# Rows of attention divided and rounded pair by pair on GpSimd, and five engines in program order

## The chip, the cores and the metric

The kernel runs on one core of one Trainium2 chip. The metric is device microseconds of a whole execution: the median of three runs was 1037.98 us (1031.45 to 1040.16). The core has TensorE (matrix products), VectorE, ScalarE, GpSimd and SyncE, each with an instruction queue of its own; in the profile they are PE, DVE, ACT, POOL and SP, and PEld is TensorE loading weights. SP issues most DMAs, ScalarE's queue issues the loads of Q, K and V, and GpSimd's queue the indirect ones.

## The reference

Attention with a threshold, followed by a mixture of experts in which each token goes to the one expert with the highest logit.

```python
# q, k, v: (8, 8, 576, 64)
scores = scale * (q @ k.T)
thresh = max(scores, axis=-1) - tau
scores = where(scores >= thresh, scores, -1e9)
attn = exp(scores - max(scores)); attn = attn / (sum(attn) + 1e-9)
x = (attn @ v) laid out as (4608, 512)          # 8 heads x 64 per token
logits = x @ w_gate                              # 8 experts
e = argmax(logits); gate = softmax(logits)[e]
out[token] = gate * (relu(x @ w1[e]) @ w2[e])
```

## The kernel before

**Tiling.** The 64 heads are worked on as 32 pairs of heads, four pairs to a batch entry (a batch in what follows, 0 to 7). A pair takes ten steps; step k of the attention loop issues one unit of transposed scores of pair n (`st_unit`: two matmul passes, an exp on ScalarE, a mask on VectorE), one unit of scores of the next pair (`s_unit`, with a row maximum on VectorE) and one piece of attention times V of the pair before (`av_piece`). Numbers are held as a high and a low half in 16 bits, so a split goes with nearly every operand: ScalarE makes the high half, VectorE or GpSimd subtracts it to get the low one. Lines: `lo` of Q and K on GpSimd (L218), the low half of V in `vop` on VectorE (L252), the low half of the exps on GpSimd (L367).

**The row maxima.** When the last score unit of a pair is done, `parts` takes the maximum of its nine columns, transposes them on TensorE (L304), splits them in three and sends them with three DMAs into the operand `CQ` that the next pair's transposed scores need (L318). `stack` copies the split Q and K with eleven or twelve DMAs of SP into the operands (L232 to L247).

**The end of a batch.** When the last of a batch's four pairs has left PSUM, `finish` takes the reciprocals of the sums (L442) and divides and splits the batch in blocks of 128 tokens by 512 columns, four blocks, five in every other batch (the rest of 64 tokens of two batches makes one). For each block `one` multiplies on GpSimd (L456; in the last batch three blocks on VectorE), ScalarE makes the high half (L463), GpSimd the low one (L464), both in the row buffer `R`, and SP transposes the block by DMA (L471). `logits` multiplies the transposed blocks with the gate's weights, `route` finds the expert and the running count (L516 to L527), `ranks` each token's position (L531 to L548), and each block is sent by an indirect DMA of GpSimd to its place in the DRAM buffer `xs` (L556). `R` is one buffer of five blocks, `xT` holds transposed ones.

**The experts.** After batch 5, 6 and 7 `tables0`, `tables1` and `tables2` find which blocks of 128 tokens are whole, and `fetch` brings a block back from `xs` (L756) and transposes it (L759). `gemm1` and `gemm2` (L804, L831) run over 32 blocks and a few late ones. Weights are loaded by SP and split by ScalarE and VectorE (L722, L723).

**Order.** The program plans everything by steps: `after(k, f, where)` puts f into the step k from now, at its front, middle or end; `phase(p, least)` gives the next step that is p modulo ten. PSUM has five score banks, two for attention times V and one (`ps_m`) that L304's transpose, the logits, the ranks and the tables take in turn. Up to step KM = 304, which is 16 before the end of the 320 steps, the queue of TensorE keeps program order; the other engines' queues are put in order by the planner of the language, which runs a timeline of its own. After KM it orders all five.

```python
        with tc.manual_schedule(engines={mybir.EngineType.PE}):
            while k < KM:
                one_step()
```

## Time and profile before

| | |
|---|---|
| median of 3 runs | 1037.98 us (1031.45 to 1040.16) |
| the profiled execution | 1028.81 us, its span 1027.1 us |
| mean granted TensorE clock | 0.978 |
| busy: PE, PEld | 933.3, 662.2 us |
| busy: DVE, ACT, POOL | 685.9, 612.2, 493.9 us |

The rows below are of this one execution. Times in a row are microseconds from the span's start. "PEclk" is the granted clock of TensorE as a share of 2.4 GHz, which is the upper of its two levels; the lower is 1.2. In a timeline the idle time of an engine just before an instruction stands in brackets at the end, with what ended it. A name such as L252 is a line of the kernel.

### The profile page before, as it was taken

To read this page: it belongs to the slowest core of one execution; us is meant where nothing else is said; L and a number is where in the kernel's file an instruction comes from. 1 tells how busy PE (TensorE), PEld (TensorE's weight loads), DVE (VectorE), ACT (ScalarE), POOL (GpSimd) and SP (SyncE) were. 2 spreads that over 40 slices of the span, in tenths; PEclk is the share of its full clock that TensorE was granted. 3 is DMA by queue.
4 is the path that set the end of the run, shared out by engine and by line. 5 is a ranking of instruction groups with operands and counts; after the bars stand their busy time and mean duration, and the time that the engine had idled before them with its cause. 6 is when DMAs were issued, how large, how long until landed. Compare 5 with 4: busy or idle time off the path is not lost.

```text
span 1027.1 us, 25249 instructions
## 1 busy us (share of the span) xinstructions
PE 933.3 (91%) x10027; PEld 662.2 (64%) x10027; DVE 685.9 (67%) x1316; ACT 612.2 (60%) x1002; POOL 493.9 (48%) x411
## 2 busy tenths in 40 slices
...
GB/s 199 141 130 114 105 154 103 148 156 115 157 152 116 141 149 122 181 122 118 121 148 136 86 134 305 285 117 249 235 161 158 234 141 178 160 155 219 218 101 26
DMA packets 181716, 158.97 MB, mean 155 GB/s; under 512 B 137561, under 2 KB 153947, under 8 KB 181596
## 3 DMA queue, kind: packets, MB, share of 16 engines
...
## 4 chain that ended last, share of the span: by engine, by line
PE 48%; DMA 20%; DVE 10%; issue 8%; ACT 7%; POOL 3%; SPq 2%; POOLq 0%; ACTq 0%; DVEq 0%
PE h L804 15%; PE y L831 12%; DMA qkf<-in_qk_dram 5%; DMA CQ<-hi 4%; PE av L405 4%; PE st L330 3%; PE s L281 3%; PE st L331 3%; PE s L283 3%; DMA wf<-in_w_dram 2%; DMA out_dram<-o,gt 2%; DVE nm L293 2%; DVE vop L252 2%; DVE e L361 2%; PE av L399 2%
## 5 line engine op out<-in xcount | busy, mean ns | idle before, releaser
L367 POOL TENSOR_TENSOR pl<-e,ph 128x1024 f16<-128x1024 f32 x95 | 202.7, 2135 | 130.7 <-ACT ph L366 54.3
L293 DVE TENSOR_REDUCE nm<-s 128x1 f32<-128x512 f32 (+1 forms) x320 | 200.3, 633 | 29.9 <-PE s L283 27.9
L804 PEld LDWEIGHTS <-wb 128*128 128x128 f16 x2304 | 191.1, 99 | 31.5 <-issue 10.6
L804 PE MATMUL h<-xTm,wb 128*128 128x256 f16 (+2 forms) x2112 | 197.6, 256 | 12.5 <-DMA xTm<-R 10.1
L831 PE MATMUL y<-wb,hl 128*128 128x512 f16 (+1 forms) x1056 | 203.9, 362 | 0.0
L281 PE MATMUL s<-QK 128*128 128x512 f16 (+3 forms) x640 | 139.5, 295 | 37.2 <-DMA QK<-lo 19.2
L831 PEld LDWEIGHTS <-hl 128*128 128x128 f16 (+1 forms) x1056 | 94.4, 100 | 99.0 <-issue 4.1
L723 DVE SCALAR_TENSOR_TENSOR wb<-wf,wb 128x1024 f16<-128x1024 f32 x96 | 116.5, 1252 | 58.3 <-ACT wb L722 56.8
L358 ACT ACTIVATE e<-st,ntau 128x512 f32<-128x512 f32 x192 | 130.3, 684 | 40.6 <-PE st L331 35.0
L330 PE MATMUL st<-QK 128*128 128x512 f16 (+3 forms) x640 | 138.0, 292 | 11.1 <-DVE e L361 8.2
L283 PE MATMUL s<-ck,CQ 128*128 128x512 f16 (+3 forms) x640 | 143.8, 293 | 1.8 <-DMA QK<-hi 1.8
L361 DVE SCALAR_TENSOR_TENSOR e<-st,e 128x512 f32<-128x512 f32 x192 | 129.8, 678 | 18.3 <-ACT e L358 17.3
L331 PE MATMUL st<-CQ,ck 128*128 128x512 f16 (+3 forms) x640 | 132.9, 289 | 3.4 <-DMA CQ<-ptT 3.4
L792 ACT ACTIVATE hl<-h 128x512 f16<-128x512 f32 (+1 forms) x80 | 45.7, 573 | 120.9 <-PE h L804 120.9
L722 ACT ACTIVATE wb<-wf 128x1024 f16<-128x1024 f32 x96 | 97.7, 1050 | 33.3 <-DMA wf<-in_w_dram 17.7
...
L405 PE MATMUL av<-vf,e 128*128 128x65 f32 (+1 forms) x1024 | 116.3, 251 | 0.0
L343 DVE SCALAR_TENSOR_TENSOR e<-st,e 128x512 f32<-128x512 f32 (+1 forms) x160 | 91.8, 586 | 22.4 <-ACT e L342 21.7
L342 ACT ACTIVATE e<-st,ntau_f 128x512 f32<-128x512 f32 (+1 forms) x160 | 93.6, 605 | 20.5 <-PE st L331 19.2
L366 ACT CAST ph<-e 128x1024 f16<-128x1024 f32 x96 | 99.8, 1039 | 7.8 <-DVE e L361 7.2
L405 PEld LDWEIGHTS av<-vf,e 128*128 128x128 f32 (+1 forms) x1024 | 101.4, 165 | 0.4 <-issue 0.4
L409 PE MATMUL av<-vop,pl 128*128 128x65 f16 x768 | 98.3, 195 | 0.5 <-DVE pl L367 0.3
...
## 6 DMA issues: line engine op xcount, KB each, us to landing
...
```

Of the source, the lines that this page charges most:

```text
L281: nc.tensor.matmul(sc[rows, oc], d["QA"][a][:, cols], d["KB"][a][:, CH[c]], start=True, stop=False)
L283: nc.tensor.matmul(sc[rows, oc], d["CQ"][:, at:at + cols.stop - cols.start], d["CK"][a][:, CH[c]], start=False, stop=True,)
L293: nc.vector.tensor_reduce(o, sc[:, 0:width(t)], axis=AX.X, op=ALU.max, negate=True)
L330: nc.tensor.matmul(sc[rows, oc], d["KB"][a][:, cols], d["QA"][a][:, CH[c]], start=True, stop=False)
L331: nc.tensor.matmul(sc[rows, oc], d["CK"][a][:, cols], d["CQ"][:, q], start=False, stop=True)
L358: nc.scalar.activation(pf, sc, AF.Exp, bias=ntau, scale=0.125 / SS)
L361: nc.vector.scalar_tensor_tensor(pf, sc, 0.0, pf, ALU.is_ge, ALU.mult)
L367: (nc.vector if (n, t) in PLV else nc.gpsimd).tensor_tensor(l, pd, h, ALU.subtract)
L405: nc.tensor.matmul(av[rows, a], d["Pf"][t][:, q], vf[:, tv], start=False, stop=last)
L723: nc.vector.scalar_tensor_tensor(o[:, :, 1], x, SW, o[:, :, 0], ALU.mult, ALU.subtract)
L804: nc.tensor.matmul(o, Wt[:, c, wh, f], x, start=c == 0 and z == 0, stop=c == 3 and z == 2,)
L831: nc.tensor.matmul(o, h[:, hh], Wt[:, f, wh, c], start=f == 0 and z == 0, stop=f == 7 and z == 2)
```

## The change

A pair is divided and rounded as soon as it has left PSUM. `evac` copies attention times V to `y`, `divide` takes the reciprocals of that pair and multiplies on GpSimd (on VectorE for the very last pair), `rounded` has ScalarE write the high half and the same engine the low half straight into the pair's columns of the row buffer. The half block of two batches is done in `lone`. `finish` is left with the transposes (`turn`), one a step, from seven steps after the batch's last pair has left PSUM (two in the last batch), and with the logits. The row buffer is doubled (`Rs`, `Rh`, `xhs`). The low half of V goes from one VectorE instruction to two of GpSimd. In `route` the count `got` moves into PSUM, and nine instructions go three to a step in place of two (`dense`). L304's transpose comes three steps after its maximum instead of two, the logits and ranks sit in the seventh step of a pair instead of the sixth, the exp buffer of tag `pf` has three places instead of four. And the program's order holds for all five queues up to KM.

The diff, without the hunks that only tell `fetch` which row buffer it may use, and that drop a name no longer used:

```diff
--- before.py
+++ after.py
@@ -44,7 +44,7 @@
 CAP = NTOK
 
 TUNE = dict(
-    lead=10, cast=1, sl=8, ll=15, sp0=6, sps=0, lv=-9, sv=-2, av=2, g=3, l=3, d=3, lg=2, g5=3, l5=3, d5=2, g6=1, l6=2, d6=2, g7=1, l7=1, d7=1, off=2, off5=1, off6=11, lg7=13, km=16, rate=15, dh=1, do=3, ws0=6, wsd=3, w1d=5, plv=1, xv=3, so=0, sto=0, ord=0, sc=5, fa=3, fd=4, wa1=-70, wa2=-86, wl1=-28, wl2=-6, avb=2, route=1, ranks=7, pp=8, ew=4, maskat=0, w1a=-40, w1b=3,
+    lead=10, cast=1, sl=8, ll=15, sp0=6, sps=0, lv=-9, sv=-2, av=2, tr=4, d=2, lg=5, d5=2, d6=2, d7=1, lg7=9, km=16, rate=15, dh=1, do=3, ws0=6, wsd=3, w1d=5, plv=1, xv=3, so=0, sto=0, ord=0, sc=5, fa=3, fd=4, wa1=-70, wa2=-86, wl1=-28, wl2=-6, avb=2, route=1, ranks=7, pp=8, ew=4, maskat=0, w1a=-40, w1b=3,
 )
 
 
@@ -191,6 +191,11 @@
             i += slot[0] > FRONT and k == 0
             after(k + i // 2, f, END if i % 2 else MID)
 
+    def dense(k, where, fs):
+
+        for i, f in enumerate(fs, where):
+            after(k + i // 3, f, i % 3)
+
     def due(k, where):
         slot[0] = where
         q = acts.get(k)
@@ -249,9 +254,9 @@
     def split_v(n):
         vop, x = vops[n % NB], vfs[n % NB][:, 0:NV, 0:D]
         nc.scalar.activation(vop[:, :, 0:D], x, AF.Copy, scale=SV)
-        after(1, lambda: nc.vector.scalar_tensor_tensor(
-            vop[:, :, D + 1:2 * D + 1], x, SV, vop[:, :, 0:D], ALU.mult, ALU.subtract
-        ))
+        full = op.tile([P, NV, D], F32, tag="full", name=f"full_{n}", bufs=2)
+        nc.gpsimd.tensor_scalar(full, x, SV, None, ALU.mult)
+        after(1, lambda: nc.gpsimd.tensor_tensor(vop[:, :, D + 1:2 * D + 1], full, vop[:, :, 0:D], ALU.subtract))
 
     def blocks(t):
 
@@ -319,7 +324,7 @@
                     st[n]["CQ"][64 + p:65 + p].rearrange("p (t c) -> p t c", t=9), t[:, p]
                 )
 
-        after(2, turn, FRONT)
+        after(3, turn, FRONT)
 
     def st_unit(n, t):
         d = st[n]
@@ -336,7 +341,7 @@
             elif "pe" in d:
                 pf = d.pop("pe")[:, 1]
             else:
-                d["pe"] = pp.tile([P, 2, 512], F32, tag="pf", name=f"e_{n}_{t}", bufs=4)
+                d["pe"] = pp.tile([P, 2, 512], F32, tag="pf", name=f"e_{n}_{t}", bufs=3)
                 pf = d["pe"][:, 0]
             d["Pf"][t] = pf
             nc.scalar.activation(pf, sc, AF.Exp, bias=ntau_f, scale=0.125 / SS)
@@ -369,15 +374,17 @@
         return mask
 
 
-    xt = {}
     sent = set()
     W = D + 1
-
-    def x_tiles(b):
-        if b not in xt:
-            half = xt[b - 1][1] if b % 2 else xp.tile([P, H, W], F32, tag="xh", name=f"xh_{b}")
-            xt[b] = (xp.tile([P, NT, H, W], F32, tag="x", name=f"x_{b}"), half)
-        return xt[b]
+    Rs = [rpool.tile([P, NT, ROW], I32, name=f"R_{i}") for i in range(2)]
+    Rh = [rpool.tile([P, ROW], I32, name=f"Rh_{i}") for i in range(2)]
+    xhs = [rpool.tile([P, H, W], F32, name=f"xh_{i}") for i in range(2)]
+
+    def row(b, j):
+        return Rs[b % 2][:, j] if j < NT else Rh[b // 2 % 2]
+
+    def halves(x):
+        return x.bitcast(F16).rearrange("p (c h d) -> p c h d", c=4, h=2)
 
     def av_piece(n, a, i):
 
@@ -409,75 +416,96 @@
             nc.tensor.matmul(av[rows, a], l, vop[:, tv, 0:W], start=False, stop=False)
             nc.tensor.matmul(av[rows, a], h, vop[:, tv, 0:W], start=False, stop=last)
         if a and i in (2, 3):
-
-            def evac():
-                x4, xh = x_tiles(b)
-                av = d["av"][i // 3 * 3][:, 0:6 * W].rearrange("p (i a c) -> p i a c", i=3, a=2)
-                hs = slice(2 * hp, 2 * hp + 2)
-                if i == 2:
-                    nc.scalar.copy(x4[:, 0:3, hs, :], av)
-                else:
-                    nc.scalar.copy(x4[:, 3, hs, :], av[:, 0])
-                    half = slice(64 * (b % 2), 64 * (b % 2) + 64)
-                    nc.scalar.copy(xh[half, hs, :], av[half, 1])
-                    if hp == 3:
-                        finish(b)
-
-            after(1, evac, FRONT)
-
-    R = rpool.tile([P, 5, ROW], I32, name="R")
-    Rf = R.bitcast(F32)
-
+            after(1, lambda: evac(n, i), FRONT)
+
+    EPS = 1e-9 * SV / SX
+
+    def divide(x, y, rs, eng):
+        wait = int(eng is nc.gpsimd)
+        nc.scalar.activation(rs, y[..., D:W].squeeze(y.ndim - 1), AF.Copy, bias=EPS)
+        after(wait, lambda: nc.vector.reciprocal(rs, rs))
+        after(2 * wait, lambda: eng.tensor_tensor(
+            x, y[..., 0:D], rs.unsqueeze(rs.ndim).to_broadcast(list(x.shape)), ALU.mult
+        ))
+
+    def evac(n, i):
+        d = st[n]
+        b, hp = divmod(n, 4)
+        av = d["av"][i // 3 * 3][:, 0:6 * W].rearrange("p (i a c) -> p i a c", i=3, a=2)
+        hs = slice(2 * hp, 2 * hp + 2)
+        if i == 2:
+            d["rs"] = small.tile([P, NT, 2], F32, tag="rs", name=f"rs_{n}", bufs=2)
+            d["y"] = xp.tile([P, NT, 2, W], F32, tag="y", name=f"y_{n}", bufs=2)
+            d["x"] = xp.tile([P, NT, 2, D], F32, tag="xn", name=f"xn_{n}", bufs=2)
+        rs, x, y = d["rs"], d["x"], d["y"]
+        lone = n == NPAIR - 1
+        eng = nc.vector if lone else nc.gpsimd
+
+        def go(js):
+            divide(x[:, js], y[:, js], rs[:, js], eng)
+            after(0 if lone else 3, lambda: rounded(b, hp, x, js, eng))
+
+        if i == 2:
+            nc.scalar.copy(y[:, 0:3], av)
+            if lone:
+                after(0, lambda: go(slice(0, 3)))
+            return
+        half = slice(64 * (b % 2), 64 * (b % 2) + 64)
+        nc.scalar.copy(y[:, 3], av[:, 0])
+        nc.scalar.copy(xhs[b // 2 % 2][half, hs], av[half, 1])
+        after(0, lambda: go(slice(3 if lone else 0, 4)))
+        if hp == 3:
+            finish(b)
+
+    def rounded(b, hp, x, js, eng):
+        o = Rs[b % 2][:, js, 0:DM].bitcast(F16).rearrange("p j (c h d) -> p j c h d", c=4, h=2)[:, :, hp]
+        x = x[:, js].rearrange("p j u d -> p j (u d)")
+
+        def low():
+            eng.tensor_tensor(o[:, :, 1], x, o[:, :, 0], ALU.subtract)
+
+        def high():
+            nc.scalar.copy(o[:, :, 0], x)
+            after(1, low)
+
+        after(int(eng is nc.gpsimd), high)
 
     def finish(b):
-        x = str(b) if b >= B - 3 else ""
-        gap, lag, dist = (TUNE[z + x] for z in "gld")
-        off = TUNE["off" + x] if b < B - 1 else 2
+        last = b == B - 1
         n = NT + b % 2
-        x4, xh = x_tiles(b)
-        rs = small.tile([P, 5, H], F32, tag="rs", name=f"rs_{b}", bufs=2)
-        eps = 1e-9 * SV / SX
-        fs = [
-            lambda: nc.scalar.activation(rs[:, 0:NT].unsqueeze(3), x4[:, :, :, D:W], AF.Copy, bias=eps),
-            lambda: nc.vector.reciprocal(rs[:, 0:NT], rs[:, 0:NT]),
-        ]
+        xTs = {}
+
+        def lone():
+            o = halves(Rh[b // 2 % 2][:, 0:DM])
+            y = xhs[b // 2 % 2]
+            rs = small.tile([P, H], F32, tag="rsh", name=f"rsh_{b}", bufs=1)
+            xn = xp.tile([P, H, D], F32, tag="xn", name=f"xnh_{b}", bufs=2)
+            x = xn.rearrange("p (c u) d -> p c (u d)", c=4)
+            eng = nc.vector if last else nc.gpsimd
+            divide(xn, y, rs, eng)
+
+            def high():
+                nc.scalar.copy(o[:, :, 0], x)
+                after(1, lambda: eng.tensor_tensor(o[:, :, 1], x, o[:, :, 0], ALU.subtract))
+
+            after(1 if last else 4, high)
+
+        def turn(j):
+            if j % 2 == 0:
+                xTs["t"] = rpool.tile([P, 2, 8, P], F16, tag="xT", name=f"xTg_{b}_{j}", bufs=3)
+            xTs[j] = xT = xTs["t"][:, j % 2]
+            nc.sync.dma_start_transpose(xT, row(b, j)[:, 0:DM].bitcast(F16))
+
         if n > NT:
-            fs += [
-                lambda: nc.scalar.activation(rs[:, NT].unsqueeze(2), xh[:, :, D:W], AF.Copy, bias=eps),
-                lambda: nc.vector.reciprocal(rs[:, NT], rs[:, NT]),
-            ]
-        chain(0, fs)
-        xTs = {}
-
-        def one(j):
-            xr = x4[:, j] if j < NT else xh
-            x = xp.tile([P, DM], F32, tag="xn", name=f"xn_{b}_{j}", bufs=2).rearrange("p (h d) -> p h d", h=H)
-            eng = nc.vector if (b, j) in XV else nc.gpsimd
-            eng.tensor_tensor(
-                x, xr[:, :, 0:D], rs[:, j].unsqueeze(2).to_broadcast([P, H, D]), ALU.mult
-            )
-            x = x.rearrange("p (c u) d -> p c (u d)", c=4)
-            Rv = R[:, j, 0:DM].bitcast(F16).rearrange("p (c h d) -> p c h d", c=4, h=2)
-
-            def high():
-                nc.scalar.copy(Rv[:, :, 0, :], x)
-                eng.tensor_tensor(Rv[:, :, 1, :], x, Rv[:, :, 0, :], ALU.subtract)
-                after(lag, turn)
-
-            def turn():
-                if j % 2 == 0:
-                    xTs["t"] = rpool.tile([P, 2, 8, P], F16, tag="xT", name=f"xTg_{b}_{j}", bufs=3)
-                xTs[j] = xT = xTs["t"][:, j % 2]
-                nc.sync.dma_start_transpose(xT, R[:, j, 0:DM].bitcast(F16))
-
-            after(lag, high)
-
+            after(1 if last else 2, lone)
+        t0 = 2 if last else TUNE["tr"] + 3
         for j in range(n):
-            after(off + gap * j, lambda j=j: one(j))
-        d = off + gap * (n - 1) + 2 * lag
+            after(t0 + j, lambda j=j: turn(j))
+        d = t0 + n - 1
+        dist = TUNE[f"d{b}"] if b >= B - 3 else TUNE["d"]
         after(
-            d + TUNE["lg7"] if b == B - 1 else phase(6, d + TUNE["lg"]), lambda: logits(b, n, xTs, dist),
-            END if b == B - 1 else FRONT,
+            d + TUNE["lg7"] if last else phase(7, d + TUNE["lg"]), lambda: logits(b, n, xTs, dist),
+            END if last else FRONT,
         )
 
     def logits(b, n, xTs, dist):
@@ -492,12 +520,13 @@
                 )
 
         Lj, w = (lg[:, z:z + n * E].rearrange("p (j e) -> p j e", e=E) for z in (128, 192))
+        got = lg[:, 256:256 + E]
         after(1, lambda: nc.vector.tensor_reduce(
             Lj, lv.rearrange("p j h e -> p j e h"), axis=AX.X, op=ALU.add
         ), FRONT)
-        after(TUNE["route"], lambda: route(b, n, dist, Lj, w))
-
-    def route(b, n, dist, Lj, w):
+        after(TUNE["route"], lambda: route(b, n, dist, Lj, w, got), FRONT)
+
+    def route(b, n, dist, Lj, w, got):
 
         bc = [P, n, E]
 
@@ -510,22 +539,31 @@
         tt = nc.vector.tensor_tensor
         mx, mw, oh, ex, sm = t2("mx"), t2("mw"), t3("oh", F16), t3("ex"), t2("sm")
         was = small.tile([P, E], F16, tag="was", name=f"was_{b}", bufs=2)
-        got = small.tile([P, E], F32, tag="got", name=f"got_{b}", bufs=2)
         posi = small.tile([P, 5], I32, tag="posi", name=f"posi_{b}", bufs=2)
-        chain(0, [
+        nc.scalar.copy(was, run)
+        dense(0, MID, [
             lambda: nc.vector.tensor_reduce(mx, Lj, axis=AX.X, op=ALU.max),
             lambda: tt(w, Lj, mx.to_broadcast(bc), ALU.is_equal),
             lambda: tt(ex, Lj, mx.to_broadcast(bc), ALU.subtract),
             lambda: tt(w, w, rank8.unsqueeze(1).to_broadcast(bc), ALU.mult),
             lambda: nc.vector.tensor_reduce(mw, w, axis=AX.X, op=ALU.max),
             lambda: tt(oh, w, mw.to_broadcast(bc), ALU.is_equal),
-            lambda: nc.scalar.copy(was, run),
             lambda: nc.vector.tensor_reduce(got, oh.rearrange("p j e -> p e j"), axis=AX.X, op=ALU.add),
-            lambda: nc.scalar.copy(
-                R[:, 0:n, DM + 1:DM + 2], tid[:, b // 2, 4 * (b % 2):4 * (b % 2) + n].unsqueeze(2)
-            ),
             lambda: tt(run, run, got, ALU.add),
+            lambda: ids(b, n),
         ])
+
+        def ids(b, n):
+            t = tid[:, b // 2]
+            nc.scalar.copy(Rs[b % 2][:, :, DM + 1:DM + 2], t[:, 4 * (b % 2):4 * (b % 2) + NT].unsqueeze(2))
+            if n > NT:
+                nc.scalar.copy(row(b, NT)[:, DM + 1:DM + 2], t[:, 8:9])
+
+        def gate(b, n):
+            c = 1.0 / (SX * SW * SW)
+            nc.scalar.activation(Rs[b % 2].bitcast(F32)[:, :, DM:DM + 1], sm[:, 0:NT], AF.Copy, scale=c)
+            if n > NT:
+                nc.scalar.activation(row(b, NT).bitcast(F32)[:, DM:DM + 1], sm[:, NT], AF.Copy, scale=c)
 
         def ranks():
             nc.scalar.activation(ex, ex, AF.Exp, scale=1.0 / (SX * SG))
@@ -546,7 +584,7 @@
                 lambda: nc.vector.tensor_reduce(pos, ps, axis=AX.X, op=ALU.add),
                 lambda: nc.vector.reciprocal(sm, sm),
                 lambda: nc.vector.tensor_copy(posi[:, 0:n].unsqueeze(2), pos),
-                lambda: nc.scalar.activation(Rf[:, 0:n, DM:DM + 1], sm, AF.Copy, scale=1.0 / (SX * SW * SW)),
+                lambda: gate(b, n),
             ]
             if b == 0:
                 fs.append(lambda: nc.vector.tensor_copy(pos0, pos[:, 0]))
@@ -554,16 +592,16 @@
 
             def send(j):
                 nc.gpsimd.indirect_dma_start(
-                    xs[:, :], bass.IndirectOffsetOnAxis(ap=posi[:, j:j + 1].bitcast(U32), axis=0), R[:, j, :], None
+                    xs[:, :], bass.IndirectOffsetOnAxis(ap=posi[:, j:j + 1].bitcast(U32), axis=0), row(b, j), None
                 )
                 sent.add((b, j))
 
             if b in TABLES:
-                after(phase(6, 6 + dist * n), TABLES[b], FRONT)
+                after(phase(7, 6 + dist * n), TABLES[b], FRONT)
             for j in range(n):
                 after(6 + dist * j, lambda j=j: send(j))
 
-        after(phase(6, TUNE["ranks"]), ranks, FRONT)
+        after(phase(7, TUNE["ranks"]), ranks, FRONT)
 
 
     def to_int(x, shape, nm):
@@ -1099,7 +1136,7 @@
                 chunk[0] += 1
             k += 1
 
-        with tc.manual_schedule(engines={mybir.EngineType.PE}):
+        with tc.manual_schedule(engines={mybir.EngineType.PE, mybir.EngineType.DVE, mybir.EngineType.Activation, mybir.EngineType.Pool, mybir.EngineType.SP}):
             while k < KM:
                 one_step()
         while busy:
```

## Rows read from the trace of the kernel before

**Rows 1.** The page's first part: busy us (share) and instructions of each engine.

```profile
PE 933.3 (91%) x10027; PEld 662.2 (64%) x10027; DVE 685.9 (67%) x1316; ACT 612.2 (60%) x1002; POOL 493.9 (48%) x411
```

**Rows 2.** Busy time by stage: length, PE, PEld, DVE, ACT, POOL, PEclk, DMA.

```profile
56.73:518.68 461.95, 436.13 (x5564) 314.94 (x5564) 406.46 (x800) 367.37 (x646) 317.92 (x184) 0.99 0.57 132
518.68:692.00 173.32, 146.04 (x1780) 107.53 (x1779) 110.46 (x258) 87.45 (x147) 74.46 (x65) 0.93 0.64 177
692.00:1027.00 335.00, 326.10 (x2520) 229.33 (x2520) 127.96 (x168) 129.78 (x171) 75.43 (x97) 0.99 0.59 172
```

**Rows 3.** Timeline of TensorE, the transpose of L304 (32 in all): start, duration, instruction.

```profile
56.73 0.28 PE L304 MATMUL pst<-ident,r 128*9 128x128 f32 x1 [1.88 <-DVE r L300]
...
88.53 0.27 PE L304 MATMUL pst<-ident,r 128*9 128x128 f32 x1
104.32 0.27 PE L304 MATMUL pst<-ident,r 128*9 128x128 f32 x1
...
518.68 0.27 PE L304 MATMUL pst<-ident,r 128*9 128x128 f32 x1
...
563.30 0.27 PE L304 MATMUL pst<-ident,r 128*9 128x128 f32 x1
```

**Rows 4.** Timelines of GpSimd, VectorE and TensorE at 470 us; L252 without company.

```profile
470.69 2.05 POOL L456 TENSOR_TENSOR xn<-x,rs 128x512 f32<-128x512 f32 x2
472.69 2.12 POOL L367 TENSOR_TENSOR pl<-e,ph 128x1024 f16<-128x1024 f32 x1
...
471.39 3.85 DVE L252 SCALAR_TENSOR_TENSOR vop<-vf,vop 128x384 f16<-128x384 f32 x1
...
475.43 0.21 PE L281 MATMUL s<-QK 128*128 128x64 f16 x1 [3.32 <-DVE nm L293]
...
193.17 0.54 DVE L252 SCALAR_TENSOR_TENSOR vop<-vf,vop 128x384 f16<-128x384 f32 x1
```

**Rows 5.** Busy time in two slices of 25 us, columns as in rows 2.

```profile
475.00:500.00 25.00, 24.57 (x275) 17.61 (x275) 21.16 (x39) 17.84 (x32) 23.24 (x16) 0.88 0.54 108
525.00:550.00 25.00, 18.82 (x216) 12.73 (x215) 23.05 (x41) 17.59 (x29) 11.12 (x8) 0.86 0.57 172
```

**Rows 6.** Groups by line and shape: count, busy us, mean ns, idle before.

```profile
L367 POOL TENSOR_TENSOR pl<-e,ph 128x1024 f16<-128x1024 f32 x95 | 202.7, 2135 | 130.7 <-ACT ph L366 54.3 <-issue 20.2 <-PE av L405 17.8
L218 POOL TENSOR_TENSOR lo<-qkf,hi 128x1152 f16<-128x1152 f32 x31 | 76.8, 2479 | 30.6 <-ACT hi L217 20.0 <-DMA ck<-lo 9.1 <-DMA CQ<-ptT 1.4
L252 DVE SCALAR_TENSOR_TENSOR vop<-vf,vop 128x384 f16<-128x384 f32 x32 | 41.2, 1291 | 0.6 <-ACT vop L251 0.6
L464 POOL TENSOR_TENSOR R<-xn,R 128x512 f16<-128x512 f32 x33 | 38.2, 1164 | 5.5 <-ACT R L463 5.3
L556 POOL DMA_INDIRECT xs<-R,posi x36 | 37.4, 1038 | 38.6 <-DMA xs<-R,posi 17.8 <-ACT ph L366 8.2 <-PE st L330 3.9
L527 DVE TENSOR_TENSOR run<-run,got 128x8 f16<-128x8 f16 x8 | 4.8, 600 | 0.0
L89 POOL TENSOR_SCALAR_AFFINE_SELECT before<-ones 128x128 f16<-128x128 f16 x1 | 0.3, 282 | 0.0
```

**Rows 7.** Timeline of GpSimd: a send behind the landing of the one before.

```profile
192.66 0.98 POOL L556 DMA_INDIRECT xs<-R,posi  x1 [3.77 <-DMA xs<-R,posi]
```

**Rows 8.** Waits of SP's queue: waiting line and releaser, us in total, times, longest.

```profile
SPq L471 <- POOL R L464: 25.3, 13, 4.9
```

**Rows 9.** Timeline of TensorE: three of its waits after 518 us.

```profile
541.00 0.37 PE L304 MATMUL pst<-ident,r 128*9 128x128 f32 x1 [5.74 <-DVE posi L548]
...
666.17 1.55 PE L804 MATMUL h<-xTm,wb 128*128 128x128 f16 x13 [6.29 <-DMA xTm<-R]
...
692.62 2.69 PE L804 MATMUL h<-xTm,wb 128*128 128x128 f16 x24 [3.39 <-DMA xTm<-R]
```

**Rows 10.** Timelines of VectorE and SP: reciprocal and last transpose of batch 7.

```profile
610.43 0.34 DVE L442 RECIPROCAL rs<-rs 128x32 f32<-128x32 f32 x1
...
627.69 1.45 SPq L471 DMA_TRANSPOSE xTg<-R  x1
```

13 lines of the change are left out of this document (6 added, 7 removed).

## The prediction

> **What bounds the kernel now.** I read the page's first part, then busy time by stage, then the cadence of the attention pairs, then what ended TensorE's idle time, and last the engine that was behind it.
>
> TensorE is busy 91% of the span [rows 1]. Cut into three stages [rows 2], the expert stage from 692 us on is TensorE alone: 326 of 335 us, the others far below. In the attention stage TensorE is busy 436 of 462 us and VectorE 406, ScalarE 367, GpSimd 318: no engine is full on average, so the loss has to be looked for in places.
>
> The cadence shows it. Each pair has one small transpose on TensorE (line 304), so its starts are a clock for pairs. From 56.73 to 518.68 there are 27 intervals, a mean of 461.95 / 27 = 17.11 us. An interval in which TensorE did not visibly wait, 88.53 to 104.32, takes 15.79 [rows 3]. A step is a tenth of that, about 1.6 us. So up to 1.3 us a pair, 35 us in all, is lost to waits.
>
> One such wait, in full [rows 4]: from 470.69 to 474.8 GpSimd does two divisions and a low-half subtraction back to back. VectorE starts the low half of V (line 252) at 471.39 and needs 3.85 us; the same instruction took 0.54 us at 193.17. Its queue stands behind it, the row maxima with it, and TensorE waits 3.32 us for them at 475.43. So an instruction of VectorE with two SBUF inputs stands still while GpSimd runs two-input work. Over all 32 pairs it has a mean of 1.29 us [rows 6], so 32 x (1.29 - 0.54) = 24 us of VectorE time is standing, mostly where batches are divided, because then GpSimd has no gaps. Each long wait is paid twice: the slice from 475 to 500 has a granted clock of 0.88 [rows 5]. Between the levels 1.2 and 2.4 GHz that is 24% of 25 us, 6 us, at the low level, and 3 us of work lost.
>
> **The change part by part.** *Low half of V moved to GpSimd.* It takes 32 x 1.29 = 41.2 us off VectorE [rows 6] and adds two GpSimd instructions a pair of 384 columns. No row has this first one (one input, one constant). Bounds: a one-input GpSimd instruction of 128 columns took 0.28 us, not less for 384; at the two-input rate of line 464, 1.164 / 512 x 384 = 0.87 us. I take 0.87 for both, as the rate has rows at three sizes: 1.7 us a pair, 56 us in all. It hides in GpSimd's idle time, 144 us of the attention stage [rows 2], and the result is wanted more than ten steps later.
>
> The Trainium skill (GPSIMD Engine Reference, section 3.1) speaks against this edit: two-input elementwise work belongs on VectorE, GpSimd is about twice as slow. The rows agree, 0.54 us against 0.87 for the same 384 columns; by the rule alone the edit costs 32 x (1.74 - 0.54) = 38 us of engine time instead of gaining. It is time lost only if GpSimd becomes the bound, the second rival.
>
> *Rows divided pair by pair.* The same columns are divided, rounded and subtracted, four to five blocks of 512 at two GpSimd instructions of about 1.1 us, but not in one burst. A burst pair before has 6.4 + 2.5 us of line 367 and 218 [rows 6], up to five blocks at 2.2 = 11, and sends at 1.04, four of them: 24 us against 17.1. It has to spill over. After: 8.9 + 2.2 + 1.7 = 12.8 in an ordinary pair, 80% of 16 us; with five sends 18, a spill of some 2 us that the next pair takes up. The reciprocal and ScalarE's copy of the sums come per pair instead of per batch: +0.6 us a batch on each, beside 15% and more idle time; nothing.
>
> *Running count.* `got` goes to PSUM, so the sum at line 527 has one SBUF input and can't stand still; about 3 us over the kernel, counted in the cadence.
>
> *Doubled row buffer.* The next batch's rows needn't wait until the sends of the last have landed (a send waits 3.77 us for the one before it [rows 7]). Counted in the cadence too.
>
> *Order.* Four more queues in program order. The order by hand gives the transposes (SP) two steps after their last subtraction; before, SP stood 25.3 us behind line 464 in 13 waits [rows 8], with the stacked Q/K copies behind it. The risk: ScalarE, VectorE or SP waits with ready work behind. Bounds: nothing below; above 1.3 us a pair, as much as all waits cost now. I take 0.4 us a pair, 11 us, nearer to nothing, since every consumer sits one to three steps behind its producer, each of 1.6 us against instructions of 0.6 to 2.5 us. *Three instead of four exp buffers*: the new one is wanted two steps after the last matmul on the oldest; nothing, or 1 us a pair if TensorE is late by two steps. *The small transpose one step later*: its rows still have four steps until the next pair; nothing.
>
> *Term 1, attention.* 17.11 down to 15.79 + 0.4 = 16.2: 27 x 0.91 = **24.6 us**.
>
> *Term 2, 518.68 to 563.30.* Two pairs at 22.3 us [rows 3]. In one TensorE waits 5.74 us for line 548, the ranks of batch 5, whose PSUM buffer the transpose needs [rows 9]; the slice around it has clock 0.86 [rows 5], 3.5 us lost. The new order has those ranks nine steps earlier (step 277 instead of 286) and keeps transposes and ranks in different steps. The first expert's weights still load VectorE there. I take the wait and a third of the clock: **7 us**.
>
> *Term 3, 563 to 692.* The last batch runs from its reciprocal at 610.43 to its last transpose on SP at 627.69 [rows 10]; then five sends, and TensorE waits 6.29 and 3.39 us for rows of the experts [rows 9]. After, three of the four pairs are already rounded and VectorE has about 1,000 columns left, so the transposes come some 8 us sooner. What comes earlier is eaten in part by the five sends, each behind the landing of the last [rows 7], which stay. I take two thirds of 9.7: **6 us**.
>
> The start and the expert stage: nothing, as neither's work changes. Against that, **5 us** for new waits at both edges of the ordered stretch. Sum: 24.6 + 7 + 6 - 5 = 32.6, about 32. The profiled execution took 1028.8 us (span 1027.1 and 1.7 around it) and would take 997. The median shown is 9.2 us above it: 1037.98 - 32 = **1006 us**.
>
> **The rivals.** *All waits go.* Every pair at 15.79 (35 us), the wait and the whole clock loss of term 2 (9) and the 9.7 us of term 3 with 4 of clock: 58 us, 980. For it: it's all in the rows. Against it: four engines at 80 to 95% of a pair in fixed order leave jitter, and a batch's logits and ranks are matmuls too, which the interval of 15.79 doesn't hold. Chance 0.13.
>
> *GpSimd becomes the bound.* It decides once its work in a pair passes the cadence: 12.8 us and 18 in a pair with sends, more if sends wait for landings (3.77 us each [rows 7], in order now, with the lows behind). Five such waits make 18 + 5 x 2 = 28 us in one pair of four; the average is then (3 x 12.8 + 28) / 4 = 16.6 and bursts push the pairs to 17: term 1 falls to 3, with 7 - 5 + 3 from the others 8 us, **1030**. The rule of the Trainium skill (GPSIMD Engine Reference, section 3.1) would end here. Chance 0.15.
>
> *Slower: SP stands still.* SP's queue carries the transposes, eleven stacked copies and the rows of maxima of each pair in fixed order. If a low half on GpSimd is over two steps (3.2 us) late, the transposes wait and the copies behind them; beyond about four steps TensorE waits as well. Seven batch ends at, say, the 4.9 us of [rows 8] plus 3 us of clock [rows 5] are 7 x 7.9 = 55 us against the 24.6 + 7 + 6 = 38 gained: +17, **1055**. Against it: in the average pair GpSimd has 3 us of air. Chance 0.12.
>
> **How the numbers follow.** Forecast 0.60, all waits go 0.13, GpSimd bound 0.15, slower 0.12. The forecast's own range is 990 to 1022, by order costs between 0 and 0.8 us a pair and half or all of terms 2 and 3. The range of 8 in 10 takes in part of the first rival and nearly all of the second: 985 to 1036. About 1% is what a measurement can tell here, 10 us. Faster (below 1027.6) is the forecast and the first rival, 0.73; same is the second, 0.15; slower the third, 0.12.
>
> **What would show it.** Cadence of line 304's successor: about 16.2 us, no interval over 18 before the weight splits. No VectorE instruction over 1 us before them. GpSimd busy near 370 us of the attention stage. No wait for line 548's successor. Last transposes sooner after the last row copy. It's wrong if SP waits for GpSimd grow with TensorE's waits for QK or CQ, if an engine's queue stands behind a send, or if TensorE's pairs stay near 17 though VectorE is free.

## The result: 1023.5 us, a third of the gain that was forecast

| | before | changed |
|---|---|---|
| median (range) | 1035.4 us (1025.7 to 1040.2, 6 runs) | 1023.5 us (1023.2 to 1025.1, 6 runs) |
| profiled execution, span | 1028.8, 1027.1 us | 1023.4, 1021.6 us |

The ratio is 0.9897, with an interval of 0.9849 to 0.9945: 12 us faster where 32 were forecast. The direction was right and the time lies in the range; the size was wrong. One thing about the table: the executions of the kernel before spread over 15 us and the profiled one lies 6.6 us below their median, while those of the changed kernel lie within 2 us. So the two traces, which are all that a ledger can be made of, differ by 5.5 us and not by 12.

The ledger goes by the same marks in both traces (before by [rows 3, 9]). "Last copy" is where ScalarE begins its last copy of attention's sums out of PSUM, "first send" the first of the last batch's five sends, "steady expert work" TensorE's first expert matmul after its last long wait for gathered rows.

| stretch | before | changed | gained | forecast |
|---|---|---|---|---|
| start to the third small transpose | 56.73 | 52.81 | 3.9 | 0 |
| 27 intervals | 461.95 | 462.22 | -0.3 | 24.6 |
| the next two pairs | 44.62 | 40.97 | 3.7 | 7 |
| from there to the last copy | 42.9 | 50.2 | -7.3 | |
| last copy to first send | 44.9 | 27.2 | 17.7 | 6 (with the next) |
| first send to steady expert work | 41.6 | 43.4 | -1.9 | |
| from there to the end of the span | 334.5 | 344.8 | -10.3 | 0 |
| sum | 1027.1 | 1021.6 | 5.5 | 32.6 with -5 for new waits |

At the last copy the two kernels are level, 606.2 us in both: whatever was gained before it is lost again by then. What the change gains lies between the last copy and the first send, and more than half of that is given back in the expert work.

The page's first part after the change answers to [rows 1]: VectorE has 35 us less, GpSimd 60 more, TensorE the same.

```profile
PE 931.8 (91%) x10027; PEld 661.2 (65%) x10027; DVE 650.5 (64%) x1309; ACT 609.9 (60%) x1036; POOL 554.2 (54%) x477
```

Busy time by stage, in the first two stretches of [rows 2] and from the steady expert work on (PE, PEld, DVE, ACT, POOL, clock, DMA). In the first, VectorE falls from 406 to 380 us and GpSimd rises from 318 to 377. The work moved as the change says, and the attention stretch is as long as before.

```profile
56.73:518.68 461.95, 433.61 (x5592) 312.72 (x5587) 380.09 (x804) 371.89 (x687) 377.12 (x244) 0.98 0.57 135
518.68:692.00 173.32, 145.73 (x1799) 111.67 (x1796) 103.65 (x250) 85.49 (x147) 82.17 (x75) 0.92 0.73 191
676.80:1021.60 344.80, 336.92 (x2640) 237.35 (x2640) 129.96 (x170) 131.70 (x174) 72.80 (x98) 0.99 0.58 168
```

The timeline of TensorE's small transpose (line 309 now) answers to [rows 3]. Of the 27 intervals, 24 have a mean of 16.19 us (15.4 to 18.2). Three are far off: 23.87 (the one shown, 198.63 to 222.50), 23.84 and 26.00. They are the pairs behind batches 1, 3 and 5, those with a half block, a fifth one. Above 16.19 they cost 7.7 + 7.6 + 9.8 = 25 us.

```profile
52.81 0.27 PE L309 MATMUL pst<-ident,r 128*9 128x128 f32 x1
...
198.63 0.27 PE L309 MATMUL pst<-ident,r 128*9 128x128 f32 x1
222.50 0.27 PE L309 MATMUL pst<-ident,r 128*9 128x128 f32 x1 [0.43 <-DVE run L552]
...
515.03 0.27 PE L309 MATMUL pst<-ident,r 128*9 128x128 f32 x1
531.46 0.27 PE L309 MATMUL pst<-ident,r 128*9 128x128 f32 x1
556.00 0.28 PE L309 MATMUL pst<-ident,r 128*9 128x128 f32 x1 [0.63 <-DVE r L305]
```

In each of the three, TensorE has done the logits of four blocks and then waits for the fifth one's transposed rows. The same timeline, line 517:

```profile
213.22 0.38 PE L517 MATMUL lg<-wg,xTg 128*128 128x16 f16 x8 [4.63 <-DMA xTg<-Rh]
...
349.92 0.38 PE L517 MATMUL lg<-wg,xTg 128*128 128x16 f16 x8 [4.70 <-DMA xTg<-Rh]
...
488.97 0.38 PE L517 MATMUL lg<-wg,xTg 128*128 128x16 f16 x8 [6.42 <-DMA xTg<-Rh]
```

Where was the fifth block? GpSimd subtracted its low half at 198.11, 1.15 us long, so it was ready at 199.26:

```profile
198.11 1.15 POOL L489 TENSOR_TENSOR Rh<-xnh,Rh 128x512 f16<-128x512 f32 x1
```

SP issued its transpose at 209.36, ten microseconds later. SP's own timeline shows why. Four transposes hold the queue for 5.57 us, then come the fill of CQ and twelve stacked copies of the next pair, 0.5 to 1.2 us each, without a gap. The fifth transpose stands behind them in program order, and behind it the last rows of CQ:

```profile
194.48 5.57 SPq L497 DMA_TRANSPOSE xTg<-R  x4
200.14 0.80 SPq L237 DMA_DIRECT2D CQ<-before  x1
201.06 1.15 SPq L243 DMA_DIRECT2D QK<-hi  x1
...
208.66 0.59 SPq L252 DMA_DIRECT2D CQ<-hi  x1
209.36 2.00 SPq L497 DMA_TRANSPOSE xTg<-Rh  x1
211.47 2.48 SPq L323 DMA_DIRECT2D CQ<-ptT  x3
```

So SP is busy from 194.48 to 213.95, 19.5 us in a row, where a pair takes 16. And the wait is paid twice, as in the kernel before [rows 5]. Busy time in slices of 4 us, with the granted clock as the third number from the right: TensorE stands for most of the second slice, in which the clock begins to fall, the third is at 0.50 (1.2 GHz), and the fourth is nearly back.

```profile
204.00:208.00 4.00, 3.62 (x81) 3.09 (x80) 3.34 (x8) 3.29 (x6) 2.75 (x2) 1.00 0.90 200
208.00:212.00 4.00, 0.58 (x24) 0.49 (x20) 0.37 (x1) 0.63 (x1) 2.98 (x3) 0.73 0.39 76
212.00:216.00 4.00, 2.78 (x21) 1.68 (x21) 0.64 (x2) 1.49 (x2) 0.00 (x0) 0.50 0.29 57
216.00:220.00 4.00, 4.00 (x34) 2.73 (x34) 3.17 (x9) 2.79 (x6) 2.37 (x1) 0.92 0.33 122
```

In the third slice TensorE works for 2.78 us at half the clock, 1.4 us of work lost; 8% of the next 4 us are 0.3. With the waits of 4.63 and 0.43 that makes 6.8 of the 7.7 us by which this interval is too long. The logits themselves cover the rest: the pairs with those of batches 0, 2 and 4, without such a wait, take 17.3 to 18.2 us.

### The profile page after: what moved, and what is told of

The parts are those of the page before. It is cut to its first block, busy times and chain, and to the rows that moved or that the text cites. A ratio compares the mean times of both kernels' runs of the same rounds, so it can differ in the third digit from the quotient of the medians.

```text
span 1021.6 us, 25156 instructions
## 1 busy us (share of the span) xinstructions
PE 931.8 (91%) x10027; PEld 661.2 (65%) x10027; DVE 650.5 (64%) x1309; ACT 609.9 (60%) x1036; POOL 554.2 (54%) x477
## 4 chain that ended last, share of the span: by engine, by line
PE 60%; DMA 14%; issue 9%; DVE 7%; ACT 5%; POOL 3%; SPq 1%; POOLq 0%; ACTq 0%; DVEq 0%
PE h L842 15%; PE y L869 12%; PE av L412 6%; PE st L335 5%; PE st L336 5%; PE s L286 5%; DMA CQ<-ptT 5%; PE s L288 5%; PE av L406 2%; DMA xs<-R,posi 2%; DMA out_dram<-o,gt 2%; DVE nm L298 2%; PE av L417 1%; PE av L416 1%; PE av L415 1%
## 5 line engine op out<-in xcount | busy, mean ns | idle before, releaser
L869 PE MATMUL y<-wb,hl 128*128 128x512 f16 (+1 forms) x1056 | 201.8, 360 | 0.8 <-issue 0.6
L412 PE MATMUL av<-vf,e 128*128 128x65 f32 (+1 forms) x1024 | 119.8, 255 | 0.0
L881 POOL DMA_INDIRECT out_dram<-o,gt x40 | 42.7, 1068 | 134.4 <-ACT o L880 115.8
L412 PEld LDWEIGHTS av<-vf,e 128*128 128x128 f32 (+1 forms) x1024 | 105.0, 168 | 0.7 <-issue 0.3
L415 PE MATMUL av<-vop,ph 128*128 128x64 f16 x768 | 98.1, 195 | 0.0
```

The lines of the kernel that those rows point to most:

```text
L412: nc.tensor.matmul(av[rows, a], d["Pf"][t][:, q], vf[:, tv], start=False, stop=last)
L869: nc.tensor.matmul(o, h[:, hh], Wt[:, f, wh, c], start=f == 0 and z == 0, stop=f == 7 and z == 2)
```

## The experiments

After the result two theories stood on the three long pairs. A: SP's queue is in program order and nearly full where a batch ends, and the fifth transpose stands behind the stacked copies. B: the half block itself is late (copied out, divided, rounded, subtracted). On the end of the kernel, D: what attention gains is swallowed behind it. Ratios are against the kernel before, run on the same chip at the same time.

| | edit | median us | ratio (interval) | 27 intervals | the three long pairs |
|---|---|---|---|---|---|
| | changed kernel | 1023.5 | 0.990 (0.985 to 0.995) | 462.2 | 23.9, 23.8, 26.0 |
| e1 | transposes a step sooner | 1023.5 | 0.988 (0.982 to 0.994) | 452.3 | 22.1, 21.6, 20.0 |
| e2 | transposes a step later | 1040.4 | 1.002 (0.999 to 1.005) | 478.5 | 24.9, 25.1, 25.3 |
| e3 | half block rounded sooner | 1022.4 | 0.985 (0.980 to 0.991) | 465.6 | 24.6, 25.3, 27.4 |
| e4 | V's low half back on VectorE | 1052.2 | 1.015 (1.010 to 1.021) | 481.4 | 25.2, 26.8, 27.8 |
| e5 | only TensorE in program order | 1029.2 | 0.993 (0.990 to 0.997) | 459.9 | 18.0, 24.0, 17.3 |
| e6 | before, V's low half on GpSimd | 1054.0 | 1.018 (1.015 to 1.021) | 484.4 | |
| e8 | order by hand 28 steps longer | 1048.2 | 1.013 (1.010 to 1.015) | 470.0 | 26.8, 26.6, 26.5 |
| e9 | fifth transpose on ScalarE's queue | 1031.4 | 0.996 (0.993 to 0.999) | 461.7 | 24.7, 24.3, 24.2 |
| e10 | logits of batches 1 and 3 a pair later | 1025.6 | 0.990 (0.984 to 0.996) | 464.6 | 19.9, 21.0, 26.7 |
| e11 | e1, gathers asked for six steps later | 1024.7 | 0.987 (0.979 to 0.994) | 456.5 | 21.0, 21.5, 21.2 |
| e12 | e11, transposes spread | 1019.5 | 0.985 (0.979 to 0.991) | 448.2 | 17.5, 17.1, 20.5 |
| e13 | before, five engines in program order | 1052.7 | 1.014 (1.007 to 1.021) | 472.7 | |
| e14 | e12, gathers really behind | 1015.4 | 0.975 (0.968 to 0.982) | 453.2 | 19.0, 17.2, 22.0 |
| e15 | e14, second expert's weights later | 1016.0 | 0.978 (0.971 to 0.984) | 454.7 | 17.2, 20.0, 21.5 |
| e16 | changed kernel, both end edits | 1029.1 | 0.989 (0.982 to 0.995) | 466.4 | 24.1, 24.3, 26.1 |
| e17 | e14, loads ahead of the gathers | 1013.4 | 0.978 (0.973 to 0.982) | 453.2 | 20.3, 17.2, 21.1 |

Profiled executions of the same attention program (e1 and e11, or e12, e14, e15 and e17) differ by 4 to 6.5 us in the 27 intervals, so differences of that size say nothing here.

### When the transposes are issued (e1, e2, e3)

e1 and e2 shift the step at which the transposes are issued; e3 leaves them and rounds the half block a step sooner.

```
e1   tr=4  ->  tr=3
e2   tr=4, lg=5  ->  tr=5, lg=4
e3   after(1 if last else 4, high)  ->  after(1 if last else 3, high)
```

> The changed kernel with the transposes of a batch one step sooner (tr 3 in place of 4), so that the fifth one, of the half block, stands on SP ahead of the next pair's stacked Q/K copies and not behind them. Theory A (SP's order: the fifth transpose waits behind 13 copies, 9 us, and TensorE's logits wait for it): the three pairs of 23.9, 23.8 and 26.0 us fall to 15.5 to 18, TensorE's waits for the transposed half block go from 15.7 us to under 2, and the time from 1023.5 to about 1000 (ratio to the kernel before 0.965 to 0.975). Theory B (the half block's low half comes late from GpSimd): the transposes now wait for GpSimd, TensorE waits as before, 1020 to 1026.

> The changed kernel with the transposes one step later (tr 5) and the logits left in the same step (lg 4). Theory A: now the fourth transpose also comes behind the stacked copies, so that the even batches' logits pairs (three in the ordered stretch) become long as well, by 5 to 9 us each: 1038 to 1052. Theory B: the half block is ready in any case by then; 1023 or a few us more.

> The changed kernel with the half block's rounding one step sooner (high after 3 steps in place of 4, the low half follows), its transpose where it was. Theory A: nothing, 1021 to 1026, and the three long pairs stay. Theory B: the half block is ready a step sooner and the three pairs shrink by about 1.6 us or more each, 1013 to 1019.

In e1 the waits for the fifth transpose are gone from the attention stretch and the 27 intervals are 10 us shorter. The three pairs stay longer than the 15.5 to 18 us expected; what is left of them is a wait of 3 us for the rows of CQ, the next thing in SP's queue. TensorE's timeline of e1:

```profile
216.43 0.58 PE L336 MATMUL st<-CQ,ck 128*128 128x512 f16 x1 [3.00 <-DMA CQ<-ptT]
...
352.08 0.58 PE L336 MATMUL st<-CQ,ck 128*128 128x512 f16 x1 [2.95 <-DMA CQ<-ptT]
```

In e2 the fourth transpose slips behind the copies as well, and now the pairs behind batches 0, 2 and 4 are long too (21.6, 24.1, 23.1 us): six long pairs in place of three, +16 us. TensorE's timeline of e2, a wait behind batch 0 and one behind batch 2:

```profile
143.74 0.36 PE L517 MATMUL lg<-wg,xTg 128*128 128x16 f16 x8 [2.56 <-DMA xTg<-R]
...
288.81 0.38 PE L517 MATMUL lg<-wg,xTg 128*128 128x16 f16 x8 [4.34 <-DMA xTg<-R]
```

In e3 the half block is ready 4.4 us sooner (its low half begins at 193.67 us) and TensorE waits as long for its transpose as before, 4.84 us at the first place. B falls. Of A, the effect of the queue's order is shown by e1 and e2 in both directions; but e1's time is that of the changed kernel, so 10 us of attention were lost further on.

```profile
212.66 0.38 PE L517 MATMUL lg<-wg,xTg 128*128 128x16 f16 x8 [4.84 <-DMA xTg<-Rh]
```

### The parts one by one (e4, e5, e6, e13)

e4 and e5 undo one part in the changed kernel; e6 and e13 make one part in the kernel before (e6 with the three exp buffers of the change, to make room for the new tile).

```
e4, in the changed kernel
-        full = op.tile([P, NV, D], F32, tag="full", name=f"full_{n}", bufs=2)
-        nc.gpsimd.tensor_scalar(full, x, SV, None, ALU.mult)
-        after(1, lambda: nc.gpsimd.tensor_tensor(vop[...], full, vop[...], ALU.subtract))
+        after(1, lambda: nc.vector.scalar_tensor_tensor(vop[...], x, SV, vop[...], ALU.mult, ALU.subtract))
e5   manual_schedule(engines={PE, DVE, Activation, Pool, SP})  ->  engines={PE}
e6   e4 the other way round, in the kernel before; pf bufs=4  ->  bufs=3
e13  e5 the other way round, in the kernel before
```

> The changed kernel with the low half of V back on VectorE as one instruction with two SBUF inputs; all else as changed. The prediction's theory: it stands still again while GpSimd runs (mean 0.9 to 1.3 us in place of 0.54, single ones up to 4 us), with waits of TensorE for row maxima: 5 to 15 us slower than the changed kernel, 1028 to 1038. Rival C (the move only filled GpSimd, and pair-by-pair division alone removed the long standing): the same or faster, 1015 to 1025.

> The changed kernel with its work as it is, but with only TensorE in program order (as before), the other four engines ordered by the planner. If the order by hand on the other four queues is what gives the 24 short pairs their 16.2 us (as I reckoned, 0.4 us a pair), these go back to 16.6 to 17.1 us, and the three long pairs of 23.8 to 26 us, which I lay to SP's program order, go to under 19: in sum 27 intervals near 455 to 465 us and a time of 1015 to 1030 us. Rival one: the changed work alone carries the pace, and the order by hand costs only the three long pairs: short pairs stay at 16.2, time 1000 to 1012. Rival two: without the order the pair-by-pair rounding collides with the rest, pairs over 17.5 us: 1040 or more.

> The kernel before with one part of the change: V's low part in two GpSimd operations instead of one VectorE operation a pair (and the tile pf at three buffers instead of four, as the change has it, to make room). If VectorE's load is what sets the pace of a pair before the change, the 27 intervals of 461.95 us shorten by 10 to 20 us, time 1018 to 1028 us. Rival: GpSimd's bursts of five divided tiles at each batch's end (2.9 us an operation) now stand before V's low part, 2.1 us more a pair on GpSimd, and the pairs after a batch's end grow: 1040 to 1060 us.

> The kernel before with one part of the change alone: all five engines in program order until the last 16 steps. If program order by itself shortens a pair (I reckoned 0.4 us of each), the 27 intervals fall from 462 to 445 to 455 us. Rival, which I now hold for likelier: the work as it was (five divided tiles at once at each batch's end, 2.9 us each on GpSimd, and waits set with the planner's freedom in mind) stands in front of the softmax's operations on every queue, and pairs at batch ends go over 30 us: 500 us or more for the 27 intervals, 1060 to 1100 us in all.

e4: with V's low half on VectorE the changed kernel loses 27 to 29 us (by the ratios, by the medians) where 5 to 15 were expected, 19 of them in the 27 intervals. The instruction has a mean of 1221 ns in the attention stretch (groups by line and shape of e4), close to the 1291 of [rows 6] and far from the 540 it takes undisturbed [rows 4]. Dividing pair by pair alone makes its longest time shorter (2.44 us, 3.85 before), but does not stop VectorE from standing while GpSimd works.

```profile
L257 DVE SCALAR_TENSOR_TENSOR vop<-vf,vop 128x384 f16<-128x384 f32 x26 | 31.7, 1221 | 0.0
```

e6: the same move, made alone in the kernel before, costs 17 to 19 us; its rival was right, though in the kernel before a divided block takes GpSimd 1.10 and 1.16 us, not 2.9 an operation. GpSimd's burst of divisions at a batch's end now holds V's work too, and TensorE waits 8 us for the transposes. What the smaller exp buffer does alone was not tried. TensorE's timeline of e6:

```profile
241.89 0.38 PE L489 MATMUL lg<-wg,xTg 128*128 128x16 f16 x8 [8.04 <-DMA xTg<-R]
```

e13: program order alone costs 14 to 17 us. Ordinary pairs are short (15.4 to 18.1 us), and behind each of batches 1 to 5, odd or even, stands one of 22 to 23 us, in which TensorE waits 4.7 to 5.3 us for VectorE. The rival had divided tiles in front of the softmax on every queue, and 500 us in place of 472.7; the trace shows one instruction. The low half of V on VectorE (line 252) takes 6.38 us beside GpSimd's work, and the mask that TensorE waits for (line 343) stands behind it. This comes behind each of the five batches, 6.2 to 6.7 us each time: the standing of [rows 4], on a larger scale. Timelines of e13, VectorE's and then TensorE's:

```profile
196.18 6.38 DVE L252 SCALAR_TENSOR_TENSOR vop<-vf,vop 128x384 f16<-128x384 f32 x1
202.48 0.68 DVE L343 SCALAR_TENSOR_TENSOR e<-st,e 128x512 f32<-128x512 f32 x1
...
203.21 0.58 PE L330 MATMUL st<-QK 128*128 128x512 f16 x1 [5.26 <-DVE e L343]
```

e5: all but the order by hand gains 8 us, in the expected range. Two of the three long pairs go down to 18.0 and 17.3, one stays at 24.0, and the other 24 have a mean of 16.7, 0.5 us more than with the order (0.4 was my price for it, on the other side). Attention as a whole stands where it stood. The two pairs behind it lose 12 us (53.2 for 41.0), 8.17 of them in one wait of TensorE for the first expert table; the way from there to the last copy is 10 us shorter (40.6 for 50.2).

```profile
569.00 0.38 PE L309 MATMUL pst<-ident,r 128*9 128x128 f32 x1 [8.17 <-DVE row L609]
```

So the parts do not add up. Moving V alone: +17 us; order alone: +17; everything without V's move: +14; everything without the order: -8; all together: -12 (medians). V's move costs time where the divisions come in one burst (e6). The order costs time where V's low half is on VectorE, with the divisions in a burst (e13) or spread (e4). The order with V's move and without the spread was not tried.

### Whose queue, and who comes too early (e9, e10)

```
e9   nc.sync.dma_start_transpose(xT, ...)  ->  (nc.scalar if j == NT else nc.sync).dma_start_transpose(xT, ...)
e10  phase(7, d + TUNE["lg"])  ->  phase(7, d + (14 if b in (1, 3) else TUNE["lg"]))
```

> The changed kernel with the half block's transpose (the fifth of batches 1, 3, 5, 7) issued from ScalarE's queue instead of SP's, at the same place in program order. If SP's queue in program order is the bound of the three long pairs, TensorE's logits waits of 4.63, 4.70 and 6.42 us go under 1 us and the pairs of 23.9, 23.8 and 26.0 us fall to 17 to 20, the 27 intervals from 462 to 443 to 452 us. If the end swallows what the ordered stretch gains, the time stays at 1017 to 1024; if not, 1004 to 1013. Rival: the transposes are late whatever queue they stand in (their data or their landing), or ScalarE loses as much standing before its own issue: pairs over 22 us, 1021 to 1030 us.

> The changed kernel with TensorE's logits of batches 1 and 3 one pair later, at the same place in the pair; the transposes stay where they are. If the pairs at 23.9 us are long because TensorE comes to the fifth transpose before it has landed, and then runs some microseconds at the lower clock, intervals 11 and 19 fall to 16.5 to 18 us with no wait over 1 us, and the next pairs grow by the 1.3 us of the logits; interval 27 (26.0 us, batch 5, left as it is) stays. 27 intervals 446 to 450 us. If SP's full queue then shows at its next consumer, as in the run with the transposes a step sooner (3 us of waiting for the last rows of CQ), intervals 11 and 19 stay at 20 to 22 us: 454 to 458 us. The time: 1008 to 1015 if the end passes the gain on, 1019 to 1024 if it swallows it.

e9 did not take the wait away; it moved it to ScalarE. There the transpose stands until a copy of SP's queue has landed, and with it the exponentials: 6.42 us. SP in its turn issues nothing from 204.67 to 207.85. TensorE then waits 4.02 us for the masks. So in this kernel the transpose on the second queue was ordered against the first queue's transfers, and e9 can't separate "SP is full" from "the transpose is late". ScalarE's timeline of e9, its queue of transfers and the next exponential:

```profile
204.33 1.39 ACTq L498 DMA_TRANSPOSE xTg<-Rh  x1
205.77 0.69 ACT L363 ACTIVATE e<-st,ntau 128x512 f32<-128x512 f32 x1 [6.42 <-DMA ck<-lo]
```

e10 moves the consumer. The two pairs fall from 23.9 to 19.9 and 21.0 us, the wait for the transpose is gone, and the rows of CQ behind it in SP's queue now set the end, 3.52 us at the first place. That is the mechanism of the second of the two expectations: the queue is full, and whoever needs its tail waits. Its sum was missed. The 27 intervals are 464.6 us and not 454 to 458: the pairs behind take the logits over (18.3 and 18.4 us), and two others wait 2.1 to 2.3 us for the rows of CQ.

```profile
217.75 0.38 PE L336 MATMUL st<-CQ,ck 128*128 128x512 f16 x1 [3.52 <-DMA CQ<-ptT]
```

### SP's work spread over two pairs (e11, e12)

e11 is e1 with the gathers of expert blocks 3 and 4 later, meant for the end (below). e12 adds to e11 a gap of three steps between the transposes of batches 0 to 4; their logits follow a pair later.

```
e11  after(1 + m, lambda m=m: fetch(NF + m))  ->  after(7 + m, ...)
e12  after(t0 + j, ...), d = t0 + n - 1  ->  gap = 3 if b < 5 else 1
                                             after(t0 + gap * j, ...), d = t0 + gap * (n - 1)
```

> The run with the transposes a step sooner (1023.5 us, 27 intervals 452 us), with one thing more: the gathers of expert blocks 3 and 4 are asked for six steps later. In that run the last half block is rounded at 602.7 us but its transpose starts at 613.45, behind the transposes of those two gathers on SP. If that queue order is what swallows the 10 us of the attention stretch, the last half block's transpose starts before 606 us, the last batch's positions stand before 622 us (628.7 there), the steady expert work begins before 670 us (677 there), and the time is 1012 to 1017 us. Rival: the weight loads and the five sends of 30 us hold it in any case, or blocks 3 and 4 now come too late for TensorE: the steady expert work still begins at 675 to 680 us, 1021 to 1028 us.

> The run with the transposes a step sooner and the gathers of blocks 3 and 4 later, with the transposes of batches 0 to 4 three steps apart instead of one, and their logits behind them (one pair later where that is needed). If a full SP queue in the pair that follows a batch's end is the bound there, spreading its 5.6 to 7 us of transposes over two pairs leaves intervals 11 and 19 at 16.5 to 18 us, interval 27 (batch 5, close together) at 20, no wait over 1 us for the rows of CQ, and 27 intervals at 441 to 447 us. Rival: what is spread meets the rows of CQ in every pair instead, and pairs that stood at 15.4 to 16.4 us grow by 0.5 to 1 us: 450 us or more. The time follows the run before this one minus the gain, 1003 to 1012 us, if the end passes it on; 1018 to 1026 if it does not.

With the transposes spread, the pairs behind batches 1 and 3 take 17.5 and 17.1 us, and TensorE waits at most 1.94 us in them; the one behind batch 5, whose transposes stay together, takes 20.5. The 27 intervals are 448.2 us, 14 less than in the changed kernel. In e14, e15 and e17, with the same attention program, they are 7 to 9 us less, and one of the two pairs is still at 19.0 to 20.3 us, with a wait of 1.9 to 3.1 us for the rows of CQ. With e10, which moved the logits alone, this shows the cause of the long pairs: SP's transposes and stacked copies in one pair. Little of the gain reaches the end: the median is 4 us below the changed kernel's, in the range named for a gain that is swallowed (the profiled execution, the fastest of four, has a span 7.4 us below).

### The end (e8, e11, e14, e15, e16, e17)

```
e8   while k < KM:  ->  while k < KEND + 12:      (the part under manual_schedule)
e14  e12 with after(12 + m, lambda m=m: fetch(NF + m))
e15  e14 with w1a=-40  ->  w1a=-32
e16  the changed kernel with the edits of e14 and e15 to fetch and w1a
```

> The changed kernel with all five engines kept in program order 28 steps further, over the last 16 steps of attention and 12 steps beyond, where the planner ordered them. If the planner's mixing of the last batch's routing and sends with weight splits and loads is what keeps the steady expert work from beginning before 677 us, the stretch from pst[31] to there shortens: time 1008 to 1018 us. Rival: program order puts work that could run ahead behind work that waits, the stretch grows by more than 5 us: 1028 to 1050 us.

> The run with spread transposes (1019.5 us; its last rows are copied out at 590.9 us, its steady expert work begins at 669.4), with the gathers of expert blocks 3 and 4 asked for another five steps later: now they stand behind the last half block's transpose on SP, which they did not in the two runs before. If SP and GpSimd, each in its order, make the last transposes and the gathers wait for one another, the last half block's transpose starts before 601 us (607.5 there), the last logits before 605 (610.8), and the steady expert work begins 4 to 7 us sooner: 1012 to 1016 us. Rival: the routing of the last batch stands behind the weight splits on VectorE in any case (5.2 us at 617.9 there): positions still at 621 to 624 us, time 1017 to 1022.

> The run before this one, with the loads and splits of the second expert's weights eight work items later. If VectorE's wait for a weight split in the middle of the last batch's routing (5.2 us) and ScalarE's splits ahead of the gate are what else holds the sends, the time from the last logits to the first send falls from 16.5 us to 8 to 11 us, the steady expert work begins before 661 us, and the time is 1005 to 1012. Rival: the weights are then late for the second expert, TensorE waits for them after 680 us, 5 us or more: 1014 to 1022.

> The changed kernel with only those two edits to its end (gathers of blocks 3 and 4 eleven steps later, the second expert's weights eight items later), its transposes as they are. The attention stretch stays as it is (27 intervals 460 to 465 us). If the end can be shortened by order alone, the steady expert work begins before 670 us (676.8 in the changed kernel), 1012 to 1018 us. Rival: in the changed kernel the last half block's transpose is not held up (3.3 us behind its rounding), so the edits gain nothing: 1021 to 1027.

e8: more order by hand is worse, by 25 us against the changed kernel. Its last copy comes at 644.6 us, 38 later than there; behind the copy the way to the steady expert work is 62 us and not 71. The planner's order is not simply at fault.

The rest is told by four moments in each trace: when ScalarE begins the last copy of attention's sums, when SP issues the last half block's transpose (before: the last transpose, [rows 10]), when the first of the last five sends is issued, when the steady expert work begins.

| | last copy | last transpose | first send | steady | copy to send | send to steady |
|---|---|---|---|---|---|---|
| before | 606.2 | 627.7 | 651.1 | 692.6 | 44.9 | 41.6 |
| changed | 606.2 | 615.1 | 633.4 | 676.8 | 27.2 | 43.4 |
| e1 | 597.3 | 613.5 | 633.9 | 677.2 | 36.6 | 43.4 |
| e11 | 601.7 | 617.5 | 638.2 | 680.1 | 36.5 | 41.9 |
| e12 | 590.9 | 607.5 | 627.4 | 669.4 | 36.5 | 42.1 |
| e14 | 599.5 | 608.2 | 627.4 | 672.5 | 27.9 | 45.1 |
| e15 | 597.2 | 606.7 | 625.3 | 670.2 | 28.1 | 44.9 |
| e16 | 610.0 | 618.7 | 637.9 | 682.9 | 27.9 | 45.0 |
| e17 | 596.6 | 605.2 | 623.5 | 666.3 | 26.9 | 42.8 |

In e1, e11 and e12 the way from the last copy to the first send is 36.5 us, in the changed kernel 27.2. These 9.3 us are what e1 had gained. SP's timeline of e12 shows where they are: the last half block's transpose stands behind that of a gathered block (line 798), and this one waits until GpSimd's gather has landed.

```profile
592.45 7.86 SPq L497 DMA_TRANSPOSE xTg<-R  x4
604.91 2.54 SPq L798 DMA_TRANSPOSE R<-R  x1
607.54 1.27 SPq L497 DMA_TRANSPOSE xTg<-Rh  x1
```

e11's edit of six steps had left that order as it was. With eleven steps (e14) the half block goes first, and the way is 27.9 us. SP's timeline of e14:

```profile
601.05 7.00 SPq L497 DMA_TRANSPOSE xTg<-R  x4
608.15 1.29 SPq L497 DMA_TRANSPOSE xTg<-Rh  x1
612.80 1.24 SPq L798 DMA_TRANSPOSE R<-R  x1
```

So the swallowing in e1, e11 and e12 is explained: attention ended sooner, one of the two gathers stood ahead of the last transpose, and 9 us were gone. Why the planner put it there is not shown. In the changed kernel both gathers are behind already, and e16 gains nothing there; its rival was right, though the time, 1029.1, is 2 us above its range.

e14's rival was right too, in part: the positions are no sooner than it said (626 us). VectorE stands 6.5 us in the middle of the last routing, before a weight split. e15 did not move that split (5.1 us there, first send 28.1 us behind the copy), so its expectation fell; nor does TensorE wait for weights after 680 us, as its rival had it. VectorE's timeline of e14:

```profile
617.34 0.16 DVE L553 TENSOR_TENSOR run<-run,lg 128x8 f16<-128x8 f16 x1
623.98 1.22 DVE L762 SCALAR_TENSOR_TENSOR wb<-wf,wb 128x1024 f16<-128x1024 f32 x1 [6.47 <-ACT wb L761]
625.12 0.20 DVE L580 TENSOR_TENSOR rk<-rk,base_e 128x40 f32<-128x40 f32 x1
```

The split waits for its load, and the load stands on SP behind the transposes of the two gathers. e17 changes that place alone:

```
e17  e14 with after(22 + m, lambda m=m: fetch(NF + m))
```

> The run with the gathers really behind (1015.4 us), with the gathers of expert blocks 3 and 4 asked for another ten steps later: on SP three weight loads now go between the last half block's transpose and the transposes of these two gathers. In that run VectorE stood 6.5 us in the middle of the last routing, before a weight split whose loads SP issued only behind the gathers. If these late loads are what holds the routing, VectorE's wait there falls under 2 us, the way from the last copy of attention's sums to the first send goes from 27.9 to 21 to 24 us, and the steady expert work begins that much sooner after the copy (73.0 us there, 66 to 70 here): 1009 to 1014 us. Rival: TensorE now waits for the two gathered blocks themselves, or the sends grow by what the loads take: steady expert work 72 us or more behind the copy, 1014 to 1020 us.

VectorE's wait before the split is gone (0.85 us for TensorE is left behind it), and the positions come 22.5 us behind the last copy (26.8 in e14). VectorE's timeline of e17, the same split:

```profile
615.62 0.16 DVE L553 TENSOR_TENSOR run<-run,lg 128x8 f16<-128x8 f16 x1
615.85 1.23 DVE L762 SCALAR_TENSOR_TENSOR wb<-wf,wb 128x1024 f16<-128x1024 f32 x1
617.93 0.21 DVE L580 TENSOR_TENSOR rk<-rk,base_e 128x40 f32<-128x40 f32 x1 [0.85 <-PE rk L577]
```

Only 1 us of these 4.3 reaches the first send, because the next engine now stands in the same way: on ScalarE the gates, without which no row can go, are behind a split that waits 5.08 us for its load.

```profile
621.57 1.06 ACT L761 ACTIVATE wb<-wf 128x1024 f16<-128x1024 f32 x1 [5.08 <-DMA wf<-in_w_dram]
```

From the first send on it is 2.3 us shorter, so that the steady work begins 69.6 us behind the copy in place of 73.0. The time is in the range expected, the first send is not (26.9 us behind the copy, 21 to 24 expected).

The last column hardly moves in the nine kernels of the table: 42 to 45 us from the last batch's first send to the steady expert work. It is no constant (36.5 us in e8, 50.2 in e13). Five sends, a gather between them and the gathers of the last blocks make it up. What each of these sends waits for beyond the landing of the one before was not tried.

The best versions are e14, e15 and e17, equal within their intervals: 1013.4 to 1016.0 us, 2.2 to 2.5% below the kernel before and, by the medians, 7 to 10 us below the changed one.

## Why the prediction was right and wrong

**The cadence, right in 24 of 27, in part by luck.** I forecast 16.2 us a pair, and 24 intervals have a mean of 16.19. It was put together from 15.79 for a pair without waits and 0.4 for the order. But the kernel before has a pair of 15.39 (73.14 to 88.53), the changed one has several, and by e5 the order takes 0.5 us off these 24 pairs and adds nothing. So 16.19 is another sum than the one forecast: pairs with logits, 17.3 to 18.2 us, raise it, and the order lowers it.

The mechanism of V's move was right. VectorE's instruction that stood is gone: none of VectorE's in the 27 intervals is over 1 us, the running count takes 163 ns where it took 600 [rows 6], e4 prices the move at 27 to 29 us in the changed kernel, and e13 shows the standing at its worst. GpSimd did not become the bound: 377 us busy against about 370 forecast. The two new instructions in the groups by line and shape of the changed kernel:

```profile
L258 POOL TENSOR_SCALAR full<-vf 128x384 f32<-128x384 f32 x27 | 31.5, 1168 | 2.2
...
L259 POOL TENSOR_TENSOR vop<-full,vop 128x384 f16<-128x384 f32 x27 | 24.1, 894 | 0.0
```

The second is at the rate I took from line 464 (0.87); the first is 1.17 in place of 0.87, 8 us more over the stretch, hidden in GpSimd's idle time as the rest is. By the Trainium skill (GPSIMD Engine Reference, section 3.1) such work belongs on VectorE, with GpSimd about twice as slow. The trace agrees on the single instruction (0.54 against 0.89 us) and not on this kernel: e4 follows the rule and takes 1052 us.

**The order, wrong: the step that failed.** "Every consumer sits one to three steps behind its producer", and so 0.4 us a pair, 11 us. That looked at the steps in the program text and not at SP's queue. I reckoned SP's transposes by what they wait for [rows 8], and never added up what SP itself issues in a pair at a batch's end: five transposes at 1.3 to 2.0, thirteen copies at 0.5 to 1.2 and the rows of CQ at 2.5, 19.5 us in a row where a pair has 16. The 25 us of the three long pairs are as much as the whole gain of term 1 (24.6); 3 to 6 of them are the logits' own work. My third rival had the place and the price (SP stands, 4.9 + 3 us a batch end; it was 7.6 to 9.8) but the wrong trigger: it had GpSimd's low half late by steps, and the low half was ready 10 us ahead. It struck at three batch ends, not at seven.

SP's waits in the changed kernel, in the form of [rows 8], don't show it. For GpSimd's halves SP now waits 17.1 us (25.3 before; the name given is that of a later GpSimd instruction), less than before:

```profile
SPq L497 <- POOL full L258: 17.1, 8, 3.4
```

**Term 2, half.** Two pairs gained 3.7 us, 7 were forecast. The wait for the ranks (5.74, [rows 9]) is gone as forecast. In its place TensorE waits for VectorE's masks (3.04 and 1.13 us), and the slice from 525 to 550 has the clock it had, 0.86 [rows 5]: the third of the clock did not come back. TensorE's timeline of the changed kernel:

```profile
540.35 0.19 PE L335 MATMUL st<-QK 128*128 128x64 f16 x1 [3.04 <-DVE e L366]
```

**Term 3, wrong in size, and the expert stage.** The mechanism came: the last transpose stands 12.6 us sooner (615.1 for 627.7, 8 forecast), and the steady work begins 15.8 us sooner where I took 6. But the expert stage, which I left at nothing "as neither's work changes", gives 10.3 of it back. At that moment 344.8 us of the span are left, where it was 334.5: expert work that used to run in the gaps of the last routing now runs behind it (2640 of TensorE's matmuls from 676.8 on, 2520 in the last stage of [rows 2]). The end is as long in every run of the changed kernel, 344 to 346 us, and 334 in e6. TensorE's idle time is not saved by an earlier send if there is less left to fill it. I had counted the two waits of [rows 9] as the gain (9.7 us); they were 6.29 and 3.39 and are 1.54 and 11.40.

**The start and the edges.** I gave the start nothing, and it gained 3.9 us (the wait of 1.88 in [rows 3] among it). This comes with the order: e13 is as early (52.7 us), e5 is not (55.8).

I gave the edges -5, and at the far one 7.3 us are lost. From the last small transpose to the last copy TensorE does as many matmuls as before, 625 and then 622, in 50.2 us in place of 42.9 and at a clock of 0.90 in place of 1.00 (busy time of the kernel before and of the changed one, columns as in [rows 2]):

```profile
563.30:606.20 42.90, 39.63 (x625) 33.84 (x625) 24.61 (x77) 24.31 (x50) 21.59 (x19) 1.00 0.39 84
556.00:606.20 50.20, 43.41 (x622) 37.52 (x623) 30.24 (x69) 29.56 (x58) 30.56 (x22) 0.90 0.55 109
```

VectorE stands 8.56 us for a gathered row of the experts, and the mask that TensorE waits for comes behind it. Timelines of VectorE and TensorE in the changed kernel:

```profile
564.50 0.15 DVE L800 COPY gt<-Rm 128x1 f32<-128x1 f32 x1 [8.56 <-DMA Rm<-xs,row]
...
565.30 0.64 PE L335 MATMUL st<-QK 128*64 128x512 f16 x2 [5.01 <-DVE e L348]
```

VectorE stands there for 6.7 to 9.1 us in all runs of the changed kernel with five queues in program order, and for 3.0 in e5. That the order does it is argued from this; no run moved that copy alone. Together with the 3.7 us of term 2 and the start it leaves the last copy where it was, at 606.2 us.

**The median.** Of the 12 us between medians the traces show 5.5. The rest is the 6.6 us by which the profiled execution of the kernel before lies below its median; why its executions spread by 15 us and those of the changed kernel by 2, is open.
